# Sixteen output blocks ranked behind the last gate product, and a planner's transfer rate of 300 KB/us instead of 270

## The chip, the cores and the metric

The kernel runs on one core of one Trainium2 chip. A core has a matrix engine (PE in the profile, with its weight loads as PEld), a vector engine (DVE), a scalar engine (ACT), a general engine (POOL), a queue engine that here only issues transfers (SP), and 16 DMA engines that all queues share. The metric is the device time of one execution in microseconds (us), the median of several runs.

## The reference

The input x has 2048 positions of 512 values, in bf16. It is layer-normalised once, and two branches read the result:

- **Attention branch.** q, k and v come from one product with `wqkv` (512 by 1536), in 32 heads of 16 values. Position s attends to the 8 positions s, s-2, ..., s-14. The softmax-weighted sum of v is multiplied by `wo` (512 by 512).
- **Gated branch.** A product with `w_in` (512 by 1792) and a GELU give two halves of 896 columns, z1 and z2. z2 is layer-normalised over its columns and then mixed over positions, `g = w_sp @ z2 + b_sp`, with `w_sp` of 2048 by 2048. `z1 * g` is multiplied by `w_out` (896 by 512).

The output is x plus both branches, 2048 by 512 in bf16.

## The kernel before, in words

The 2048 positions are handled in 16 blocks of 128 (index b or tb) and 4 groups of 512 (index j or tc). The stages, with their lines:

1. Layer norm of each block (lines 583 to 625), and the normalised block transposed, by PE for the first blocks and by DMA transposes for the rest (line 615).
2. Products with `wqkv` and `w_in`: V (line 649), q and k (line 667), z2 (line 748), z1 (line 792). V is written to a scratch in HBM (`vscr`, line 658), so that the 8 shifted copies that a block needs can be read back by one strided transfer.
3. Logits: DVE multiplies q with 8 shifted views of k (line 688) and adds over the heads' values (line 693). PE sums the rest (line 701), and softmax follows (lines 713 to 740).
4. **Gate products** (`g_group`, line 868): for each tc, 7 column chunks in groups of 2, 2, 2 and 1, each chunk 16 matmuls of 128 by 512 (line 879). ACT moves a group out of PSUM (line 887), DVE adds the bias (line 890) and multiplies by z1 (line 893). The weights are the transposed rows of `w_sp`, 2 MB for each tc, loaded by four DMA transposes (line 852) into one of three slots. Slot 2 lies over the buffers of the logits, and the fourth tc takes slot 0 again.
5. **Value sums** (`pv_block`, line 896): for each block, a 1 MB load of shifted v (`Vs`, line 902, four slots), a multiply by the attention weights (line 907), three adds (lines 910 and 913), and a DMA transpose of the result (line 916) into `OT`.
6. **Output blocks** (`out_block`, line 921): 4 matmuls from `OT` (line 935), 7 matmuls from z1 times g (line 944), a DVE add with the residual (`fin`, line 950), and a store (line 955). The residual `xres` (line 925) and the result `yout` have four slots each, by tb modulo 4. The last block is split into 384 and 128 columns.

No order of work is written out for these stages. All operations go to a planner (`Plan.schedule`, line 121), which works through them once, ahead of time, with an estimated duration for each. At each step it takes, for each engine, the operations whose inputs would be ready. Among those that could start within `tol` (15 ns) of the earliest, it picks the one with the lowest `prio`. So a priority decides only among operations that are ready at the same time: when nothing of lower number is ready, a higher number goes. A transfer is counted with its bytes over one shared rate (line 216, `dma_bw`, but 190 KB/us for DMA transposes, and at most 265 in the first 7 us) and a fixed latency. The result is one fixed order for each engine and for each queue. On the chip each of them runs its list in that order and waits by semaphores.

The priorities that matter here: gate products have `300 + 10*tc + fc`, so 300 to 336 (line 885). Output blocks have `250 + tb` for tb 0 to 11, and `400 + tb` for tb 12 to 15 (line 924). On DVE, gate operations have 3, `fin` has 2, the first multiply of a value sum has `10 + b`, and its adds 1.5. On SP, the `Vs` loads have 5, the `w_sp` transposes `6 + tc`, the `OT` transposes 2, the residual loads 4 and the stores 3.

Of the kernel before, what the change touches and what calls it, by code (L numbers as in the profile page):

```python
# [328 lines left out]
def build_kernel(nc, A_x, A_wqkv, A_wo, B_x, B_w_in, B_w_sp, B_b_sp, B_w_out, out, report=False, emit=True):  # L329
# [4 lines left out]
    NJ = S // 512  # L334
# [49 lines left out]
    plan = Plan()  # L384

    with ExitStack() as es:
# [5 lines left out]
        def A(name, n, o2_=0):  # L392
            return ar[:, off[name] + o2_: off[name] + o2_ + n]

        def AC(o_, dims):
            return bass.AP(tensor=ar, offset=o_, ap=[[AR, 128]] + [list(d) for d in dims])
# [10 lines left out]
        def P(bk, n, o_=0):  # L407
            return ps[:, bk.col(o_): bk.col(o_) + n]
# [55 lines left out]
        def c_mm(n):  # L464
            return max(26.0, n / 2.4 + 2.7)
# [12 lines left out]
        def dma(eng, fn, nbytes, chan, reads=(), writes=(), name="", xbar=False, prio=0.0, after=()):  # L478
            return T(eng, fn, reads=reads, writes=writes, name=name, prio=prio, after=after,
                     dma=dict(chan=chan, nbytes=nbytes, xbar=xbar))  # L480
# [440 lines left out]
        def out_block(tb):  # L921
            sx = tb % 4
            tcb = tb // 4
            pr_ = (250 if tcb < NJ - 1 else 400) + tb
            dma("sp", lambda e: e.dma_start(A("xres", 512, 512 * sx), x2[128 * tb:128 * tb + 128, :]), 128 * 512 * 2,
                ("xres", sx), writes=[("xres", sx)], name="ldxr%d" % tb, prio=4)
            parts = [(0, 512)] if tb < NB - 1 else [(0, 384), (384, 128)]
            for c0, cn in parts:
                def part(c0=c0, cn=cn):
                    bk = plan.bank("out%d_%d" % (tb, c0))  # L930

                    def mm_o(t):
                        last = None
                        for cc in range(4):
                            last = t.matmul(P(bk, cn), AC(off["OT"] + 512 * tb + 128 * cc, [[1, 128]]),  # L935
                                            AC(off["wo"] + 512 * cc + c0, [[1, cn]]), start=(cc == 0), stop=False)
                        return last
                    T("pe", mm_o, reads=[("OT", tb)] + [("wo", c) for c in range(4)], writes=[bk], est=4 * c_mm(cn),
                      name="outo%d_%d" % (tb, c0), prio=pr_)
                    for fcs in ((0, 1, 2, 3), (4, 5), (6,)):  # L940
                        def mm(t, fcs=fcs):
                            last = None
                            for fc in fcs:
                                last = t.matmul(P(bk, cn), AC(off["z1T"] + fc * S + 128 * tb, [[1, 128]]),  # L944
                                                AC(off["w_out"] + 512 * fc + c0, [[1, cn]]), start=False,
                                                stop=(fc == FC - 1))
                            return last
                        T("pe", mm, reads=[("z1T", fc, tcb) for fc in fcs] + ["w_out"], writes=[bk],
                          est=len(fcs) * c_mm(cn), name="out%d_%d_%d" % (tb, c0, fcs[0]), prio=pr_)
                    T("dve", lambda v: v.tensor_tensor(A("yout", cn, 512 * sx + c0), P(bk, cn),  # L950
                                                       A("xres", cn, 512 * sx + c0), ALU.add),
                      reads=[bk, ("xres", sx)], writes=[("yout", sx, c0)], est=152 + 1.05 * cn,
                      name="fin%d_%d" % (tb, c0), prio=2)
                    eng = "sp" if c0 == 0 else "act"
                    dma(eng, lambda e: e.dma_start(o2[128 * tb:128 * tb + 128, c0:c0 + cn],
                                                   A("yout", cn, 512 * sx + c0)),
                        128 * cn * 2, ("out", sx if c0 == 0 else 4), reads=[("yout", sx, c0)],
                        writes=[("outd", tb, c0)], name="st%d_%d" % (tb, c0), prio=3)
                part()

        for tc in range(NJ):
            ld_wT(tc)
            for pr in PAIRS:
                g_group(pr, tc)
            for b in range(4 * tc, 4 * tc + 4):
                pv_block(b)
            if tc >= 1:
                for tb in range(4 * (tc - 1), 4 * tc):
                    out_block(tb)
        for tb in range(4 * (NJ - 1), 4 * NJ):  # L970
            out_block(tb)
# [10 lines left out]
                if byname[n0] not in byname[n1].deps:  # L982
                    byname[n1].odeps.add(byname[n0])

        plan.schedule(tol=15.0, dma_bw=270.0, dma_lat=1800.0)
        if report:
            print("arena", AR, "fp", FR)
            plan.report()
# [14 lines left out]
def bass_parallel_sum__sliding_local_dilated__mixer_gmlp__prompt_kernel(  # L1003
    nc, A_x, A_wqkv, A_wo, B_x, B_w_in, B_w_sp, B_b_sp, B_w_out, out
):
    build_kernel(nc, A_x, A_wqkv, A_wo, B_x, B_w_in, B_w_sp, B_b_sp, B_w_out, out)
# [28 lines left out]
```

## Time and profile before

| what | value |
|---|---|
| median of 3 runs | 238.85 us (238.58 to 240.19) |
| the profiled execution | 238.84 us, of which 237.6 us span from first to last instruction |
| PE busy | 232.3 us, 98% of the span |
| DVE busy | 205.5 us, 86% |
| ACT, POOL busy | 97.9 us, 28.6 us |
| DMA | 43.86 MB, mean 185 GB/s |
| gate products (line 879) | from 99.3 us to 227 us on PE, output blocks among them from 136 us on |

The time of the runs is the span and 1.24 us around it. Busy time of PE has modelled ends, since matmuls are pipelined: a row's mean of 379 ns for a 128x512 matmul is longer than the distance from one start to the next. The chain of work that ended last gives that distance: eight such matmuls in 1.73 us, so 0.216 us each. Times inside the text count from the start of the span.

### The profile page before, as it was taken

Reading aid. Unit: us, or ns where it says so; the run is one execution under the profiler, and the core shown is the slowest. Engines: PE = TensorE matmul, PEld = TensorE weight load, DVE = VectorE, ACT = ScalarE, POOL = GpSimd, SP = SyncE. Lnnn points to the kernel's source line nnn. Section 1 sums busy time; section 2 is a strip of 40 time slices with the busy share of each in tenths; the row PEclk is TensorE's granted clock in tenths of the full one; section 3 lists DMA queues with packets and bytes.
Section 4 is the critical chain, followed back from the end, with each engine's and each line's share of the span. In section 5 each row is a group of like instructions: output and inputs, shape, how many; then the busy total and the mean of one; then the engine's idle time right before and its main releaser. Section 6 shows DMA issues by size and latency. Waiting matters only on the chain.

```text
span 237.6 us, 2971 instructions
## 1 busy us (share of the span) xinstructions
PE 232.3 (98%) x1116; PEld 109.1 (46%) x1136; DVE 205.5 (86%) x268; ACT 97.9 (41%) x146; POOL 28.6 (12%) x56
## 2 busy tenths in 40 slices
PE   8899999999999999999999999999999999999996
PEld 4445555545444444444444444444444444444443
DVE  4579799988997999987899989796498989999964
ACT  3398879988997995505120130101101101010110
POOL 2268410231323500000000000000000000000000
PEclk9999999999999999999999999999999999999999
DMA  5999918999147810150099999998996987996212
GB/s 148 359 336 145 253 43 187 185 241 211 57 122 263 97 59 25 44 177 0 3 235 346 297 211 255 202 206 263 285 316 190 291 216 150 303 268 191 65 46 90
DMA packets 82013, 43.86 MB, mean 185 GB/s; under 512 B 54336, under 2 KB 81360, under 8 KB 82000
## 3 DMA queue, kind: packets, MB, share of 16 engines
q1 hardware_dynamic: 80976, 41.46, 71.7%
q0 software_dynamic: 800, 2.11, 2.9%
q8 instruction: 9, 0.15, 0.3%
q10 hardware_dynamic: 224, 0.10, 0.2%
q14 instruction: 4, 0.03, 0.0%
HBM read 26.35 MB, written 4.21 MB: 129 GB/s over the span
## 4 chain that ended last, share of the span: by engine, by line
PE 96%; DMA 2%; issue 1%; SPq 1%; DVE 0%
PE ps L879 41%; PE ps L667 12%; PE ps L748 10%; PE ps L944 10%; PE ps L792 10%; PE ps L649 6%; PE ps L935 6%; DMA arena<-in_A_wqkv_dram 2%; PE ps L701 1%; PE ps L561 0%; SPq L500 0%; SPq L521 0%; DVE arena L950 0%
## 5 line engine op out<-in xcount | busy, mean ns | idle before, releaser
L879 PE MATMUL ps<-arena 128*128 128x512 bf16 x441 | 98.6, 379 | 0.4
L879 PEld LDWEIGHTS ps<-arena 128*128 128x128 bf16 x448 | 43.6, 98 | 53.3 <-issue 0.8
L887 ACT ACTIVATE arena<-ps 128x1024 bf16<-128x1024 f32 (+1 forms) x16 | 14.7, 917 | 104.7 <-PE ps L879 98.8
L907 DVE TENSOR_TENSOR arena<-arena 128x4096 bf16<-128x4096 bf16 x16 | 36.5, 2284 | 0.0
L688 DVE TENSOR_TENSOR arena<-arena 128x4096 bf16<-128x4096 bf16 x16 | 36.4, 2278 | 0.1
L910 DVE TENSOR_TENSOR arena<-arena 128x2048 bf16<-128x2048 bf16 (+1 forms) x32 | 29.9, 948 | 0.1
L667 PE MATMUL ps<-arena 128*128 128x512 bf16 x125 | 28.6, 379 | 0.2
L693 DVE TENSOR_TENSOR arena<-arena 128x4096 bf16<-128x4096 bf16 x12 | 27.4, 2284 | 0.0
L944 PE MATMUL ps<-arena 128*128 128x512 bf16 (+2 forms) x117 | 26.5, 366 | 0.1
L748 PE MATMUL ps<-arena 128*128 128x448 bf16 x128 | 26.3, 353 | 0.0
L792 PE MATMUL ps<-arena 128*128 128x512 bf16 x110 | 24.2, 379 | 0.1
L667 PEld LDWEIGHTS ps<-arena 128*128 128x128 bf16 x128 | 14.5, 113 | 13.0
L748 PEld LDWEIGHTS ps<-arena 128*128 128x128 bf16 x128 | 12.3, 98 | 11.8 <-issue 0.4
L676 ACT ACTIVATE arena<-ps 128x1024 bf16<-128x1024 f32 x16 | 16.3, 1018 | 2.7 <-PE ps L667 2.5
L944 PEld LDWEIGHTS ps<-arena 128*128 128x128 bf16 x119 | 11.4, 98 | 12.8
L890 DVE TENSOR_TENSOR arena<-arena 128x1024 bf16<-128x1024 bf16 (+1 forms) x16 | 9.9, 622 | 8.2 <-ACT arena L887 8.1
L792 PEld LDWEIGHTS ps<-arena 128*128 128x128 bf16 x112 | 11.0, 98 | 13.2
L649 PE MATMUL ps<-arena 128*128 128x512 bf16 x61 | 15.2, 380 | 1.4 <-DMA arena<-in_A_wqkv_dram 1.1
L950 DVE TENSOR_TENSOR arena<-ps,arena 128x512 bf16<-128x512 f32 (+2 forms) x17 | 11.0, 655 | 6.3 <-issue 3.5
L798 ACT ACTIVATE arena<-ps 128x1024 bf16<-128x1024 f32 (+1 forms) x16 | 14.1, 919 | 5.0 <-PE ps L792 5.0
L935 PE MATMUL ps<-arena 128*128 128x512 bf16 (+2 forms) x65 | 16.0, 366 | 0.2
L754 ACT ACTIVATE arena<-ps 128x896 bf16<-128x896 f32 x15 | 13.7, 914 | 3.9 <-PE ps L748 3.9
(61 smaller groups left out, 172.3 us busy)
## 6 DMA issues: line engine op xcount, KB each, us to landing
arena<-vscr SPq DMA_DIRECT2D x16, 1024.0 KB, 6.8
arena<-in_A_x_dram SPq DMA_DIRECT2D x31, 128.0 KB, 5.3
vscr<-arena POOLq DMA_DIRECT2D x16, 128.0 KB, 3.4
out_dram<-arena SPq DMA_DIRECT2D x15, 128.0 KB, 5.2
arena<-in_A_wqkv_dram SPq DMA_DIRECT2D x3, 512.0 KB, 6.0
arena<-in_B_w_in_dram SPq DMA_DIRECT2D x2, 448.0 KB, 5.5
arena<-in_B_w_in_dram SPq DMA_DIRECT2D x1, 896.0 KB, 5.8
arena<-in_B_w_out_dram SPq DMA_DIRECT2D x1, 896.0 KB, 4.9
```

Of the source, the lines that this page charges most:

```text
L649: last = t.matmul(P(bk, 512), xTv(b, dc), AC(off["wv"] + 512 * dc, [[1, 512]]), start=(dc == 0), stop=(dc == 3))
L667: last = t.matmul(P(bk, 512, 512 * which), AC(off["wqk"] + 2048 * which + 512 * dc + c, [[4, 128]]), AC(off["xnT"] + dc * S + 512 * j, [[1 ...
L676: T("act", lambda a: a.activation(AC(qo, [[ko - qo, 2], [1, 512]]), P(bk, 1024).rearrange("p (t n) -> p t n", t=2), ACTF.Copy, scale=0.5), ...
L688: T("dve", (lambda pbv, qb, kb: lambda v: v.tensor_tensor(pbv, qb, kb, ALU.mult))(pbv, qb, kb), reads=rd, writes=[("pb", s_)], est=c_tt(40 ...
L693: T("dve", (lambda av, bv: lambda v: v.tensor_tensor(av, av, bv, ALU.add))(av, bv), reads=[("pb", 1)], writes=[("pb", acc)], est=c_tt(4096 ...
L748: last = t.matmul(P(bk, 448, 512 * hf), xTv(b, dc), AC(off["w_in2"] + 896 * dc + 448 * hf, [[1, 448]]), start=(dc == 0), stop=(dc == 3))
L792: last = t.matmul(P(bk, 512, 512 * i), AC(off["w_in1"] + 896 * dc + 128 * fc, [[1, 128]]), AC(off["xnT"] + dc * S + 512 * j, [[1, 512]]), ...
L879: last = t.matmul(P(bk, 512, 512 * i), AC(off["z2"] + FH * sh + 128 * fc, [[1, 128]]), AC(off["wT%d" % r_] + sh * 512, [[1, 512]]), start= ...
L907: T("dve", lambda v: v.tensor_tensor(tv, tv, av, ALU.mult), reads=[("attn", b)], writes=[("Vs", sv)], est=c_tt(4096), name="pv%d" % b, pri ...
L910: T("dve", (lambda n: lambda v: v.tensor_tensor(A("Vs", n, 4096 * sv), A("Vs", n, 4096 * sv), A("Vs", n, 4096 * sv + n), ALU.add))(n), wri ...
L935: last = t.matmul(P(bk, cn), AC(off["OT"] + 512 * tb + 128 * cc, [[1, 128]]), AC(off["wo"] + 512 * cc + c0, [[1, cn]]), start=(cc == 0), s ...
L944: last = t.matmul(P(bk, cn), AC(off["z1T"] + fc * S + 128 * tb, [[1, 128]]), AC(off["w_out"] + 512 * fc + c0, [[1, cn]]), start=False, sto ...
```

## The change

Two edits. All 16 output blocks get priorities 340 to 355, above those of every gate product. And the planner counts plain transfers at 300 KB/us. No instruction is added or removed, and no buffer changes; only the order in the engines' and queues' lists can differ.

```diff
         def out_block(tb):
             sx = tb % 4
             tcb = tb // 4
-            pr_ = (250 if tcb < NJ - 1 else 400) + tb
+            pr_ = 340 + tb
...
-        plan.schedule(tol=15.0, dma_bw=270.0, dma_lat=1800.0)
+        plan.schedule(tol=15.0, dma_bw=300.0, dma_lat=1800.0)
```

## The prediction

> **What bounds the kernel now.** I read the page's totals first, then the chain of work that ended last.
>
> ```profile
> PE 232.3 (98%) x1116; PEld 109.1 (46%) x1136; DVE 205.5 (86%) x268; ACT 97.9 (41%) x146; POOL 28.6 (12%) x56
> ...
> PE 96%; DMA 2%; issue 1%; SPq 1%; DVE 0%
> ```
>
> PE is 96% of the chain. The rest is the head, where the first product waits for weights until 6.96 us. From 16.3 us on, the list of waits gives PE's matmuls 0.2 us of idle time in all, and its weight loads nothing over 0.4 us at once. PE's work is the same after the change, so a gain can come only from gaps. "Issue" is 0.6% of the chain, 1.4 us, mostly gaps of 0.05 us that any order has. I grant 0.9 us: the floor is 238.84 - 0.9 = 237.9 us. The question is whether the new order makes PE wait.
>
> Next I read the timeline of all engines near the end (start, length, instruction).
>
> ```profile
> 229.47 0.42 DVE L913 TENSOR_TENSOR arena<-arena 128x512 bf16<-128x512 bf16 x1
> ...
> 229.91 1.19 SPq L916 DMA_TRANSPOSE arena<-arena  x1
> ...
> 232.30 1.89 DVE L950 TENSOR_TENSOR arena<-ps,arena 128x512 bf16<-128x512 f32 x3 [2.42 <-issue]
> 232.70 0.64 PEld L935 LDWEIGHTS ps<-arena 128*128 128x128 bf16 x4
> 232.91 0.81 PE L935 MATMUL ps<-arena 128*128 128x384 bf16 x4
> ```
>
> The value sum of block 15 ends on DVE at 229.89, its transpose is issued at 229.91 and takes 2.4 us to land (the transposes of line 916 in this stretch: 2.4 us from issue), so it is there at 232.3. PE loads it at 232.70. **DVE's chain is 0.4 us from being the bound**, and the stages table (busy time in each stretch) shows DVE full there:
>
> ```profile
> core 0: us, PE busy (x) PEld busy (x) DVE busy (x) ACT busy (x) POOL busy (x), PEclk, DMA share, GB/s
> ...
> 148.90:173.10 24.20, 24.09 (x111) 10.98 (x112) 17.99 (x23) 2.84 (x4) 0.00 (x0) 1.00 1.05 241
> 173.10:197.30 24.20, 24.09 (x112) 10.95 (x113) 22.23 (x25) 1.62 (x2) 0.00 (x0) 1.00 0.91 255
> 197.30:226.00 28.70, 28.54 (x131) 13.02 (x133) 27.59 (x31) 3.08 (x4) 0.00 (x0) 1.00 0.75 187
> ```
>
> From 197.3 to 226 DVE works 27.59 of 28.7 us. Its slack lies earlier: 6.2 us between 148.9 and 173.1, with DMA at its limit.
>
> **PE after the change.** The gate products start at 99.46 us, by the chain. They are 4 x 7 x 16 = 448 matmuls at 0.216 us, 96.7 us, with two sums of line 701 at 0.55 us among them. With nothing else between, the last ends at 99.46 + 96.7 + 1.1 = 197.3. An output block is 11 matmuls, 2.37 us, so block 15 would start at 197.3 + 15 x 2.37 = 232.9 and PE end where it ends now. The reorder alone costs nothing, if every input is there. Three inputs come due earlier.
>
> *The rows of w_sp.* The third gate group starts at 99.46 + 2 x 24.2 + 1.1 = 148.9 instead of 153.7, the fourth at 173.1. The waits and issues of line 852: the last transpose of the third set is issued at 139.2 and lands 4.9 us later, at 144.1; of the fourth, 155.2 + 5.2 = 160.4. The margins are 4.8 and 12.7 us. The third set cannot start before the logits are summed (130.85 us), whose place on PE and DVE the output priorities do not touch. Cost: nothing, covered by these margins. If the planner put 1 MB `Vs` loads ahead of that set on SP, each would take some 3 us of the DMA engines (1024 KB at the 346 to 389 GB/s that the transfer view shows where such loads run alone); two exceed the margin, by 1.2 us.
>
> *OT.* Blocks 12 to 14 are wanted at 225.8, 228.1 and 230.5. Before, transposes 13 and 14 were issued at 222.07 and 223.93 and landed within 2.5 us, 3.5 us early or better. Block 15 is the tight one, so I count what DVE must do before its value sum ends. By 197.3 it had done seven `fin` adds (starts 138.68 to 193.45) at 0.60 us from start to start, 4.2 us. After, these go, and four more gate groups come in (before, they began at 200.28, 212.0, 223.65 and 228.2): 3 x 1.2 + 0.68 = 4.3 us. Even. Between 197.3 and 229.9 the four groups go (-4.3), and `fin` adds rise from five (blocks 7 to 11) to thirteen (block 12 ends on PE at 228.1), so +8 x 0.60 = 4.8. The sum is **+0.5 us** on DVE. One add more, if block 13's also gets in front, makes it 1.2. If none of DVE's idle time changes, OT 15 lands at 232.3 + 0.6 = 232.9 (0.1 + 0.5), wanted at 232.7: a wait of 0.2. The store of block 12, which now can stand ahead of that transpose on SP, adds its own 0.34 to 0.58 us of issue. Value taken: 0.5 us, with ends 0 and 1.5.
>
> *The residual and yout slots.* Stores and residual loads move behind 197.3. Before, the four slots were renewed every 20 us or slower; now every 4 x 2.37 = 9.5 us. A renewal is one store and one load on SP, 0.58 + 0.43 us of issue, and a landing of 2.1 to 6.2 us (line 925 in that stretch): 3.1 to 7.2 us, under 9.5. It fits when SP is free, and costs nothing then.
>
> **The rate of 300.** It shortens a 128 KB load by 0.05 us and a `Vs` load by 0.39 us in the planner's count (1,048,576 bytes at 270 or at 300 bytes per ns). On the chip nothing changes but orders. Where `Vs` loads run alone the transfer view shows 346 to 389 GB/s, so 300 is still below what they get, and orders made with it should not lean on data that is late. Before 75 us an exchange could make PE wait: bounded below by 0, above by the one early wait for weights, 1.1 us; I take 0, the row nearest being PE's 0.2 us of waits after 16.3 us.
>
> **Sum:** 238.84 + 0.5 = 239.3 us; the profiled execution is at the median (238.85).
>
> **The rivals.**
>
> *No wait at all.* The planner may let output blocks in wherever no gate product is ready, so that the priority hardly shows, or DVE uses some of its idle 6.2 us, since SP no longer stops in front of early stores. Either way PE stays full: 238.6 to 238.9. For it: SP's list of waits has 10.7 us at line 955 for line 950. Against: the sets of w_sp are in time, so gate products are ready.
>
> *DVE's chain becomes the bound (slower).* SP's list is strict, and so is DVE's. From 197 to 232 us SP's waits show it standing at the transposes of line 916 for DVE:
>
> ```profile
> SPq L916 <- DVE arena L910: 6.6, 2, 3.8
> SPq L916 <- DVE arena L950: 5.8, 1, 5.8
> SPq L916 <- DVE arena L913: 4.5, 2, 4.2
> ```
>
> If a store or residual load stands behind such a wait (4.2 to 5.8 us), a slot's renewal takes 4.2 + 1.0 + 6.2 = 11.4 to 13.0 us against 9.5. The `fin` that needs the slot comes 1.9 to 3.5 us late, DVE waits in front of it with the value sums behind it, and OT follows. Two of the three renewals of the slots so hit give 3.8 to 7 us, less the 0.4 of slack: 242.2 to 245.4, middle 243.5. The same price comes if a `Vs` load slips behind a set of w_sp once more (the set issued from 146.88 to 157.5 left DVE idle 4.3 us at 164.5). It decides from the point where DVE loses more than 0.4 us against before. For it: every filler for PE's lists is gone at the end. Against it: less traffic before 197 us, so `Vs` may be ahead.
>
> *PE slow again after a long wait.* The first eight matmuls of 128x512 in the trace took 628 ns in the mean, the later ones 379 (though the granted clock reads 1.00 all along). If a long wait brought that back, the eleven matmuls of block 15 would cost 11 x 0.25 = 2.7 us more, on top of DVE's chain: 246.2. No row shows a long wait of PE behind the head, so this has a small chance of its own. [...]
>
> *A wait inside the gate products or in the head.* Two `Vs` loads ahead of the third w_sp set (1.2 us), or an exchange early on (up to 1.1 us): 239.9 to 241.1.
>
> *Faster:* the floor of 237.9, 0.4% below; no row leaves room for over 1% (236.5).
>
> **How the numbers follow.** Forecast, with 0 to 1.5 us of wait: 0.45, at 239.3 (238.7 to 240.4). No wait: 0.17. DVE's chain: 0.25, of which 0.24 is over 1%. PE slow again: 0.04. A wait elsewhere: 0.06, 0.02 of it over 1%, where it comes on top of the tail's. Faster by a cause not seen here: 0.03. A measurement of this kernel tells about 1% from no change. So faster 0.03, within 1% 0.45 + 0.17 + 0.01 + 0.04 = 0.67, slower 0.24 + 0.04 + 0.02 = 0.30. The range goes from 238.3, which leaves out "faster" and the low end of "no wait" (0.06), to 245.0, which leaves out the top of DVE's chain and PE slow again (0.09).
>
> **What would show it.** In the changed profile, line 879 should be unbroken from 99 to 197 us and line 935 appear only behind it; the waits of PE should name nothing but line 916's transposes, at the last blocks, by under 1.5 us. Waits of line 950 on a residual load, or of DVE between 197 and 230 us adding up to over 2 us, show the slower rival. A wait at line 879 for line 852 at 149 us shows the other. The prediction is wrong if PE's chain holds over 2.4 us of DMA or DVE, or if output blocks still run before 197 us and the time moves.

## The result, and the profile after

The changed kernel takes 239.19 us (median of 20 runs, 238.56 to 241.17). The kernel before, on the same chips, takes 238.59 us (20 runs). The ratio is 1.0035, with a 95% interval of 1.002 to 1.0049. That is slower by about 0.6 us and within the 1% that was called "no change". The forecast was 239.3. Its size is right; the profile shows that its reason is not.

The page of the changed kernel, busy time and then the chain by engine:

```profile
PE 232.3 (98%) x1115; PEld 108.9 (46%) x1136; DVE 205.2 (86%) x268; ACT 97.9 (41%) x146; POOL 29.6 (12%) x56
...
PE 90%; DMA 5%; DVE 2%; issue 1%; SPq 1%; DVEq 0%
```

PE's share of the chain fell from 96% to 90%, and DMA's rose from 2% to 5%. So at one place the chain leaves PE, for 12.1 us. The chain in order of time (start, length, what) shows where:

```profile
199.60 0.57 issue
200.17 0.68 DVE arena L893
200.85 0.34 DVE arena L890
201.18 2.21 DVE arena L907
203.40 0.28 SPq L955
203.68 0.04 issue
203.72 7.08 DMA arena<-in_A_x_dram
210.81 0.03 issue
210.84 0.05 DVEq L309
210.89 0.04 issue
210.93 0.70 DVE arena L950
211.63 0.05 issue
211.68 1.04 PE ps L935 x4
```

Read it from the end. PE's seventh output block (block 6) starts at 211.68, released by a DVE add of line 950 that ended at 211.63. That add waited for a load from x, the residual of block 4, issued at 203.72 and landed 7.1 us later. The list of waits names the same three steps (engine and line, whom it waited for: total us, times, longest):

```profile
PEld ps L935 <- DVE arena L950: 0.8, 1, 0.8
DVE arena L950 <- DMA arena<-in_A_x_dram: 0.7, 1, 0.7
PE ps L935 <- DVE arena L950: 0.3, 1, 0.3
```

The first and the third are PE's only waits for DVE or DMA after 99 us. Blocks 4 and 6 share a PSUM bank in the planner's order, so block 6 cannot start before the add of block 4 has emptied it.

PE's loss is best measured between two of its own starts, because the head differs between executions: the first product (line 649) started anywhere from 6.24 to 6.96 us in the executions of this study. From the third sum of logits (line 701, near 101 us) to the last group of the last output block there is the same work in every kernel here.

| kernel | third sum starts | last group starts | between |
|---|---|---|---|
| before | 101.12 | 234.92 | 133.80 |
| changed | 100.81 | 235.07 | 134.26 |

So PE lost 0.46 us, at block 6. The chain leaves PE for much longer, but PE works through most of that time; only the part in which it stands costs anything.

The rest of the 0.6 us between the medians lies outside the span. A run of the changed kernel takes 1.41 to 1.55 us more than its span, a run of the kernel before 1.17 to 1.29 us (in the runs beside the experiments below). No run shows what this time is. It differs by up to 0.4 us between the kernels of this study, so a small difference between two medians need not be a wait of PE.

The place that the prediction named is quiet. DVE's end of the last value sum and its transpose, and then PE's last block, from the timeline of the changed kernel:

```profile
225.53 0.42 DVE L913 TENSOR_TENSOR arena<-arena 128x512 bf16<-128x512 bf16 x1
...
225.98 1.19 SPq L916 DMA_TRANSPOSE arena<-arena  x1
...
232.84 0.64 PEld L935 LDWEIGHTS ps<-arena 128*128 128x128 bf16 x4
233.06 0.81 PE L935 MATMUL ps<-arena 128*128 128x384 bf16 x4
```

The sum ends at 225.95 instead of 229.89. Its transpose took 3.9 us to land, at 229.9, and PE wants it at 232.84: 2.9 us of room, where there had been 0.4. The table of stretches shows where DVE gained:

```profile
148.90:173.10 24.20, 24.09 (x112) 11.00 (x113) 20.38 (x23) 3.76 (x5) 0.00 (x0) 1.00 1.10 280
173.10:197.30 24.20, 24.09 (x112) 10.96 (x113) 22.78 (x25) 3.69 (x5) 0.00 (x0) 1.00 0.72 206
197.30:226.00 28.70, 28.26 (x130) 12.68 (x132) 26.93 (x34) 0.48 (x1) 0.00 (x0) 1.00 0.69 191
```

From 148.9 to 173.1 us DVE (third number) works 20.38 us instead of 17.99. Its idle time there fell from 6.2 to 3.8 us.

### The profile page after: what moved, and what is told of

Same layout as the page of the kernel before. It is cut to its first block, busy times and chain, and to the rows that moved or that the text cites. A ratio compares the mean times of both kernels' runs of the same rounds, so it can differ in the third digit from the quotient of the medians.

```text
span 237.8 us, 2981 instructions
## 1 busy us (share of the span) xinstructions
PE 232.3 (98%) x1115; PEld 108.9 (46%) x1136; DVE 205.2 (86%) x268; ACT 97.9 (41%) x146; POOL 29.6 (12%) x56
## 4 chain that ended last, share of the span: by engine, by line
PE 90%; DMA 5%; DVE 2%; issue 1%; SPq 1%; DVEq 0%
PE ps L879 41%; PE ps L667 12%; PE ps L748 10%; PE ps L792 10%; PE ps L944 7%; PE ps L649 6%; PE ps L935 4%; DMA arena<-in_A_x_dram 3%; DMA arena<-in_A_wqkv_dram 2%; DVE arena L907 1%; PE ps L701 1%; DVE arena L950 1%; PE ps L561 0%; SPq L500 0%; DVE arena L893 0%
## 5 line engine op out<-in xcount | busy, mean ns | idle before, releaser
L944 PE MATMUL ps<-arena 128*128 128x512 bf16 (+2 forms) x117 | 26.9, 366 | 0.1
L935 PE MATMUL ps<-arena 128*128 128x512 bf16 (+2 forms) x66 | 16.5, 366 | 0.4 <-DVE arena L950 0.3
```

## The experiments

Two things were open: which edit did which, and whether the chain from the late residual over the add to the bank is really what PE pays for. Each kernel below was timed in turn with the kernel before on the same chip.

**The rank alone.**

```diff
-            pr_ = (250 if tcb < NJ - 1 else 400) + tb
+            pr_ = 340 + tb
```

> The output blocks rank behind the gate products, the rate stays 270. Theory A (the rate repays what the rank costs: with 300 the last logits' sum comes 7 us earlier and the value sums end 4 us earlier): without it the value sum of block 15 ends at 230 us or later, its transpose lands after 232.7, and PE waits for it before block 15; 0.5 to 2 us over the kernel before, ratio 1.002 to 1.008, so more than the whole change (1.0035). Theory B (the rank costs what the whole change costs, and the rate nothing): ratio 1.0035, PE's only wait at an early output block for line 950, as in the changed kernel, and the value sum of block 15 ends by 227 us.

238.86 us against 238.42, ratio 1.0015 (1.0006 to 1.0025). PE's stretch is 100.73 to 234.77, 134.04 us, so 0.24 us lost. The timeline has the end of the last value sum and its transpose at 270:

```profile
229.60 0.42 DVE L913 TENSOR_TENSOR arena<-arena 128x512 bf16<-128x512 bf16 x1
...
230.05 1.20 SPq L916 DMA_TRANSPOSE arena<-arena  x1
```

Counted from the third sum of logits, this value sum ends at 230.02 - 100.73 = 129.29 us, against 229.89 - 101.12 = 128.77 before: 0.52 us later. The prediction's ledger for DVE said 0.5. Yet PE does not wait for the transpose, which lands at 232.55, just when PE loads it for a block that starts at 232.76; PE had already lost its 0.24 us to a wait for line 950, and so came later itself:

```profile
PEld ps L935 <- DVE arena L950: 0.5, 1, 0.5
```

No add waits for a residual load in this kernel. The chain goes through eight DVE operations in a row, from 204.84 to 211.34 us, the last of which is the late add: it stands behind gate operations and value sums in DVE's list. So a bank can come late with no transfer being late. Theory A was wrong on the size and on the wait: the rank alone does not cost more than the whole change, and PE does not wait for the transpose. Theory B was right on the wait and wrong on the size and on the end of the value sum. Eight of the eleven matmuls of one output block also ran at 148.56 us, between the second and third gate groups, so with 270 the new rank does not put all output work behind.

**The rate alone.**

```diff
-        plan.schedule(tol=15.0, dma_bw=270.0, dma_lat=1800.0)
+        plan.schedule(tol=15.0, dma_bw=300.0, dma_lat=1800.0)
```

> The old ranks, the rate 300. Theory A: the sum of the last logits (line 701) comes at 123 us instead of 130, the value sum of block 15 ends some 2 to 4 us before 229.9, PE never waits, and the time is that of the kernel before: ratio 0.998 to 1.001. Theory B (the rate changes nothing that matters): the same time, but value sums that end at 229 to 230 us. Theory C (the rate is what costs): ratio 1.003 or more, with a wait of PE that the profile shows.

238.76 us against 238.42, ratio 1.0012 (0.9998 to 1.0027): no difference that can be told. What there is lies outside the span (1.66 us against 1.25 in the medians); the spans are 237.1 and 237.2 us. PE's stretch is 133.80 us, as before. The last sum of logits comes 7 us earlier (timeline of this kernel; 130.26 in the kernel before):

```profile
122.87 0.62 PE L701 MATMUL ps<-arena 128*32 128x512 bf16 x8
```

and the last value sum ends at 225.71. So the early value sums of the changed kernel come from the rate alone, and theory A holds on this point.

**Other banks.** In the changed kernel, an output block takes the bank that has been free longest. (The planner otherwise prefers a single bank whose neighbour is in use, and so gives the output blocks two banks in turn.)

```diff
-                    mate = 0.0 if (m["prev"] is not None and m["prev"].left > 0) else 1.0
+                    mate = 0.0 if b.name.startswith("out") or (m["prev"] is not None and m["prev"].left > 0) else 1.0
```

> The changed kernel, but each output block takes the PSUM bank that has been free longest, instead of two banks in turn. Theory A (PE's only wait, 0.45 us before output block 6, is for the bank that the late add of block 4 still holds): line 950 still waits for its residual load, but PE does not wait for line 950; ratio 1.000 to 1.002 against the kernel before. Theory B (the wait is of another origin, or the extra time is outside PE's chain): PE still waits at line 935, or the ratio stays at 1.0035.

238.58 us against 238.42, ratio 1.0006 (0.9988 to 1.0025). The waits after 99 us still hold the late residual, but no PE wait for line 950:

```profile
DVE arena L950 <- DMA arena<-in_A_x_dram: 0.5, 1, 0.5
```

PE's stretch is 133.80 us. The add is late, and PE does not feel it.

**More slots.** In the changed kernel, eight slots for residuals and eight for results, in memory that is free by then.

```diff
...
-            sx = tb % 4
+            sx = tb % 8
+            xr = A("xres" if sx < 4 else "Vn", 512, 512 * (sx % 4))
+            yo = A("yout" if sx < 4 else "D", 512, 512 * (sx % 4))
...
```

> The changed kernel with eight slots for residuals and eight for results instead of four, so that blocks 4 to 7 need no renewal. Theory A: the residual of block 4 is long there, line 950 does not wait for a load, the add of block 4 is on time and PE does not wait before block 6; ratio 1.000 to 1.002. Theory B (the residual's lateness is no cause, the bank is late for another reason, such as DVE's order): PE still waits 0.3 to 0.5 us for line 950, ratio 1.0035.

238.41 us against 238.42, ratio 0.9999 (0.999 to 1.0008). The waits have neither the load nor the bank. PE's stretch is 133.80 us. Taking away either link of the chain gives PE's 0.46 us back, so the chain is shown from both ends.

**The first renewal ahead.** In the changed kernel, the first store and the residual load of block 4 go ahead of one of the two last 1 MB loads of shifted v.

```diff
-                      ("rstd3", "Vw0"),
+                      ("rstd3", "Vw0"), ("ldxr4", "ldVs14"),
```

> The changed kernel, but the queue of SP issues the first store and the residual load of block 4 ahead of the load of shifted v for block 14 instead of behind it. Theory A (that load took 7.1 us to land instead of 2.4 because 2 MB of shifted v stood ahead of it): it lands by 209 us, line 950 does not wait for a load, PE does not wait before block 6, and PE's time from the third logits' sum to its last group is 133.8 us as in the kernel before (134.26 in the changed one); ratio 1.000 to 1.002. Theory B (such a load is slow in this stretch whatever stands ahead): line 950 still waits, ratio 1.0035.

The changed kernel's queue of SP has two such loads ahead of that pair:

```profile
200.56 1.21 SPq L902 DMA_DIRECT2D arena<-vscr  x2
201.81 1.87 SPq L955 DMA_DIRECT2D out_dram<-arena  x1
203.72 0.96 SPq L925 DMA_DIRECT2D arena<-in_A_x_dram  x1
```

and this one has one ahead:

```profile
200.51 0.52 SPq L902 DMA_DIRECT2D arena<-vscr  x1
201.07 0.58 SPq L955 DMA_DIRECT2D out_dram<-arena  x1
201.69 1.48 SPq L925 DMA_DIRECT2D arena<-in_A_x_dram  x1
203.22 0.43 SPq L902 DMA_DIRECT2D arena<-vscr  x1
```

The load is issued 2.0 us earlier and lands after 5.8 us instead of 7.1, at 207.5 instead of 210.8. Line 950 does not wait for it, PE does not wait, and PE's stretch is 100.69 to 234.49, 133.80 us. The landing itself is still far from 2.4 us: most of the gain is the earlier issue, and theory A's reason for the 7.1 us is shown only in part. The time was 238.73 us against 238.38, ratio 1.0021 (1.0006 to 1.0036), just above the expected range. Of these 0.35 us, 0.25 lie outside the span (1.48 us against 1.23 in the medians). The spans are 237.25 and 237.2 us, so they give no sign of a wait in the other executions.

**DVE's room, in the kernel before and with the rate.** One useless DVE operation, 128x4096, ahead of the last add of block 15's value sum, with every list otherwise as it was.

```diff
+        _last = byname["pvc15"].fn
+
+        def pvc15_late(v):
+            for nm, n_ in (("wT1", 4096),):
+                v.tensor_tensor(A(nm, n_), A(nm, n_), A(nm, n_), ALU.max)
+            return _last(v)
+        byname["pvc15"].fn = pvc15_late
```

> The kernel before, with one useless DVE operation of 128x4096 (2.2 us) ahead of the last add of block 15's value sum. If DVE's chain is 0.4 us from being the bound, PE waits 1.8 us before block 15: ratio 1.006 to 1.009. If the chain has more room than the trace says, 1.000 to 1.003.

240.42 us against 238.38, ratio 1.0085 (1.0066 to 1.0103). The waits after 99 us:

```profile
PEld ps L935 <- DMA arena<-arena: 2.1, 1, 2.1
PE ps L935 <- DMA arena<-arena: 1.6, 1, 1.6
```

PE's stretch is 100.73 to 236.27, 135.54 us, so 1.74 us lost of the 2.2 us put in. The kernel before really stands some 0.4 us from this bound.

> The kernel with the rate alone, with the same useless operation at the same place. If the rate gives DVE's chain 4 us of room (block 15's sum ends at 225.7 there), PE does not wait: ratio 0.999 to 1.003. If its early end is worth nothing, 1.006 to 1.009 as in the kernel before.

239.00 us against 238.38, ratio 1.0019 (1.0002 to 1.0037). PE waits for no transpose. It loses 0.44 us at another place: with the rate's order the useless work also holds up a gate operation, and block 12 waits for it.

```profile
PEld ps L944 <- DVE arena L893: 0.8, 1, 0.8
PE ps L944 <- DVE arena L893: 0.3, 1, 0.3
```

So the rate's order has the room that the kernel before lacks: the same work costs 1.74 us there and nothing here at the transpose.

**Two residual slots** in the changed kernel instead of four.

```diff
+            sr = tb % 2
...
-            dma("sp", lambda e: e.dma_start(A("xres", 512, 512 * sx), x2[128 * tb:128 * tb + 128, :]), 128 * 512 * 2,
-                ("xres", sx), writes=[("xres", sx)], name="ldxr%d" % tb, prio=4)
+            dma("sp", lambda e: e.dma_start(A("xres", 512, 512 * sr), x2[128 * tb:128 * tb + 128, :]), 128 * 512 * 2,
+                ("xres", sr), writes=[("xres", sr)], name="ldxr%d" % tb, prio=4)
...
```

> The changed kernel with two residual slots instead of four, so that a slot is renewed every 4.7 us instead of 9.5. If late renewals hold the adds, and the adds hold DVE and PSUM (the slower rival of the prediction), the first renewals, behind the last loads of shifted v, come 3 us late or more, PE waits at blocks 4 to 7, and the time is 2 to 7 us longer: ratio 1.01 to 1.03. If a late add costs PE nothing in general, it stays within 1 us of the changed kernel: below 1.008.

243.04 us against 238.38, ratio 1.0212 (1.0169 to 1.0254). The size is as expected; the place is not. PE hardly loses anything (101.05 to 234.98, 133.93 us), since the planner gave the blocks other banks: PE starts block 15 at 232.97 us, when the adds of blocks 12 to 14 have not begun, and with two banks in turn it could not. The adds fall behind instead, and end the kernel. DVE's timeline at the end (the add of line 950 is line 951 in this kernel):

```profile
228.89 1.49 DVE L951 TENSOR_TENSOR arena<-ps,arena 128x512 bf16<-128x512 f32 x2 [3.15 <-DMA arena<-in_A_x_dram]
232.32 0.69 DVE L951 TENSOR_TENSOR arena<-ps,arena 128x512 bf16<-128x512 f32 x1 [1.94 <-DMA arena<-in_A_x_dram]
...
239.08 0.76 DVE L951 TENSOR_TENSOR arena<-ps,arena 128x384 bf16<-128x384 f32 x2 [1.44 <-DMA arena<-in_A_x_dram]
```

The last adds start 4.0 us later than in the changed kernel (235.10), each behind a load that stands behind a store, which waits for the add before.

**A long wait of PE.** The kernel before, with 5.56 us of useless DVE work at the same place: as in the diff above, with one operation of 128x8192 and one of 128x2048.

> The kernel before, with useless DVE work of some 5.6 us (one operation of 128x8192, one of 128x2048) ahead of the last add of block 15's value sum, so that PE waits 5 us before block 15. If a PE that has waited that long runs slow again (the rival of the prediction), block 15's matmuls of 384 columns start further apart than the 0.163 us of the kernel before (0.65 us for four), up to twice that, and the time is 5.2 + 1.5 to 2.7 us longer. If not, 5.2 us longer and the distances are as before.

245.62 us against 238.58, ratio 1.0268 (1.0204 to 1.0333): 7.0 us longer, within the 6.7 to 7.9 expected of a PE that runs slow again. The timeline of PE, and the stretches (PE's busy time is the first number behind the length, the granted clock the third from the end):

```profile
237.42 1.46 PE L935 MATMUL ps<-arena 128*128 128x384 bf16 x4 [4.78 <-DMA arena<-arena]
238.68 2.30 PE L944 MATMUL ps<-arena 128*128 128x384 bf16 x7
240.82 0.39 PE L935 MATMUL ps<-arena 128*128 128x128 bf16 x4
241.04 0.55 PE L944 MATMUL ps<-arena 128*128 128x128 bf16 x7
```

```profile
233.00:236.00 3.00, 0.00 (x0) 0.00 (x0) 3.00 (x6) 0.00 (x0) 0.00 (x0) 1.00 0.00 0
236.00:238.00 2.00, 0.58 (x2) 0.28 (x3) 0.67 (x2) 0.00 (x0) 0.00 (x0) 0.82 0.66 178
238.00:240.00 2.00, 2.00 (x8) 0.92 (x7) 0.00 (x0) 0.00 (x0) 0.00 (x0) 0.50 0.25 84
240.00:243.00 3.00, 1.59 (x15) 1.00 (x13) 0.85 (x2) 0.00 (x0) 0.00 (x0) 0.88 0.15 42
```

After 4.8 us without work the granted clock is 0.50. Four matmuls of 384 columns take 1.26 us from group to group, against 0.65. At 240.8 the groups of 128 columns are back at their old distance of 0.22 us. From the first group's start to the last group's it is 241.04 - 237.42 = 3.62 us, against 234.92 - 232.91 = 2.01: 1.6 us more.

**The rank alone, with other banks** (both diffs above, rate 270).

> The rank alone (rate 270), and output blocks rotate over the PSUM banks. Theory A (at 270 the value sums are what runs late, as the prediction's ledger has it, and the bank wait hides a part of it): no wait of PE for line 950, but a wait for the last transpose of line 916 before block 15, 0.3 to 2 us; ratio 1.001 to 1.008. Theory B (the banks are all that the rank costs, with either rate): no wait of PE, ratio 1.000 to 1.001.

240.36 us against 238.58, ratio 1.0061 (1.0037 to 1.0084). PE's waits are those of the prediction, and the add's wait is that of its slower rival:

```profile
PEld ps L935 <- DMA arena<-arena: 2.1, 1, 2.1
PE ps L935 <- DMA arena<-arena: 1.6, 1, 1.6
DVE arena L950 <- DMA arena<-in_A_x_dram: 1.5, 1, 1.5
```

PE's stretch is 100.92 to 236.46, 135.54 us, 1.74 us lost. One add waits 1.53 us for its residual, the adds of block 15's value sum stand behind it and end at 231.84 us, and the transpose issued at 231.93 lands 2.5 us later, at 234.4, when PE starts block 15. Theory A holds as to the wait. With the rate at 270 the banks are not the cost; DVE's chain is, and most of what it loses is the late residual. Without those 1.53 us block 15 would have waited some 0.2 us (an estimate, 1.74 - 1.53), which is the wait that the prediction's ledger worked out.

**The changed kernel once more.**

> The changed kernel once more, unedited, to see whether its wait comes in another execution: a wait of PE for line 950 of 0.3 to 0.7 us before block 6, ratio 1.002 to 1.005. If the wait is of one execution only, the wait is absent or elsewhere.

238.94 us against 238.58, ratio 1.0009 (0.998 to 1.0038). The same wait is there, smaller (waits after 99 us):

```profile
PEld ps L935 <- DVE arena L950: 0.5, 1, 0.5
DVE arena L950 <- DMA arena<-in_A_x_dram: 0.4, 1, 0.4
```

The residual landed 6.9 us after its issue, and PE's stretch is 100.82 to 234.80, 133.98 us: 0.18 us lost, against 0.46 in the first execution and 0.3 expected at least. In both executions the wait is at the same place, and it is shorter where the load landed sooner. The ratio is below the expected 1.002, though its interval reaches beyond it; so the cost of the change is 0.4 us in this series of runs and 0.6 in the first, outside time included.

## Why the prediction was right in size and wrong in cause

**Right: PE's work sets the time, and the reorder alone is free.** The stretch is 133.80 us in the kernel before, with the rate alone, and in the three edits of the changed kernel that take the wait away. The w_sp rows were in time. The gate products run unbroken, and line 935 comes only behind them, from 196.99 us on.

**Right, but hidden: the ledger of DVE.** "+0.5 us" for the rank (0.6 with the stretch before 197.3) was 0.52 us where the rank ran alone, and for the reason given: thirteen adds of line 950 stand before the end of the value sum instead of twelve, and DVE's idle time from the third sum of logits to that end, 14.0 us before, stays about the same (an estimate: one add more is 0.60 us of work, and the end came 0.52 us later). The 0.4 us of room in the kernel before was confirmed: 2.2 us of extra work cost 1.74.

**Wrong: the rate as a term of nothing.** The step that failed is "I take 0" for the rate, together with the condition "if none of DVE's idle time changes". The prediction asked only whether an early exchange could make PE wait. The exchange had another effect: DVE finished the logits ahead of the first value sums, the last sum of logits came 7 us earlier, the third w_sp set was issued from 125.8 us instead of 131.0, and block 15's value sum ended at 225.95. From the third sum of logits to that end DVE is idle for 11.3 us instead of 14.0. That pays for the rank's 0.5 us several times over, so the forecast wait before block 15 was 0 in the changed kernel. That the rate does this is shown, by the run with the rate alone; which of the exchanges in the lists of DVE and SP carries it was not tested one by one.

**Missing: the PSUM banks.** The prediction counted a renewal of a residual slot at 3.1 to 7.2 us, "it fits when SP is free, and costs nothing then". SP was not free. The first store was issued 1.6 us after its add, behind two transposes and two 1 MB loads, its issue took 1.9 us, and the residual load took 7.1 us. From the end of the add to the landing that is 10.6 us, more than the 9.5 us between renewals, and the add of block 4 came 0.7 us late. The slower rival had this lateness go over DVE to OT, with a price of 3.8 to 7 us. In the changed kernel it went over the bank that blocks 4 and 6 share, a link that the prediction did not have, for 0.46 us. That it came out beside the forecast's 0.5 us is chance.

**Its own signs.** The signs on the gate products held. The others point away from the forecast. PE's one wait names line 950, not line 916's transposes, and line 950 waited for a residual load, which was to show the slower rival. DVE's waits from 197 to 230 us add up to 3.6 us, where over 2 was to show it, though half of that is one add waiting for PE near the end. The chain holds 7.1 us of DMA behind the head, where over 2.4 us of DMA or DVE was to show the prediction wrong.

**The rivals.** The slower one was no phantom. With 270 and free banks it happened as described, over OT, at 1.74 us in all, less than its price of 3.8 to 7; with two slots it cost 4.7 us, over the adds themselves. In the changed kernel the loads behind the first landed sooner (after 6.2, 5.6 and 4.5 us, then after 2.1 to 3.1), no other add waited for one, and DVE's chain had 2.9 us of room. "No wait at all" came true at the place that it named: DVE used 2.4 of its 6.2 idle us and PE did not wait for OT, though it was the rate that brought this; the wait at block 6 it did not have. "PE slow again" did not occur in the changed kernel. The run with the long wait shows that it is real, at 1.6 us where 2.7 was put. Its eleven matmuls of 384 columns took 3.40 us instead of 1.79, so 0.15 us more each, where the estimate took 0.25 from the modelled lengths of matmuls of 512 columns. The eleven of 128 columns ran at speed again.

## What to carry to other kernels

When blocks of work are moved together, everything that was renewed in the pauses between them is renewed at the pace of the block: count buffers, and PSUM banks among them, against the slowest landing that the queue can have at that moment and the time from when the buffer is free to when its renewal is issued (7.1 and 3.5 us at block 4 of the changed kernel). When a change has two edits, one of which only alters a planner's estimate, treat it as a reorder of everything behind it and look for what it could make early, not only late. And when two kernels differ by half a microsecond, measure between two fixed points of the bounding engine, since the head alone differed by 0.7 us from execution to execution, and the time outside the span by 0.4 us from kernel to kernel.

## What the runs showed of the hardware that was not expected

The clock's fall could be read from the stretches of the run with the long wait. PE's last matmul before the wait ended at 232.65 us. The granted clock reads 1.00 from 233 to 236 us, 0.82 in the mean from 236 to 238, 0.50 from 238 to 240 and 0.88 from 240 to 243. Taken as one step from 1.00 to 0.50 and one step back, these means put the fall at 237.3 us, 4.6 us after that matmul, and the return at 240.7, 3.4 us after the fall (an estimate from the four stretches). From 240.8 on the matmuls are back at full distance: four of 128 columns take 0.22 us to the next group, as in the kernel before. After waits of 1.6 us (the kernel before with 2.2 us of useless work, and the rank with other banks; mean granted clock 1.000 in both) the four matmuls of 384 columns took 0.66 us to the next group, against 0.65 in the kernel before. So the clock was at half after a wait of 4.8 us, and the matmuls kept their distance after waits of 1.6 us; at what length between the two a wait begins to cost clock, these runs do not show.

In the changed kernel a residual load of 128 KB took 7.1 us to land when it was issued close behind two 1 MB loads on the same queue, and 2.1 us at 225.3 us, when the last 1 MB load lay 24 us back. With a pace of 9.5 us for each slot, these 5 us decide whether a renewal is in time.
